# An FFT mixing layer and a GELU MLP on one core: batch 1's first stage packed closer, its filters reloaded around the read behind it, seven products in the last tile

## The chip, the cores and the metric

The kernel runs on one core of a Trainium2 chip. The metric is the device time of one execution in microseconds, the median of seven runs. Of the core's engines, PE multiplies matrices into PSUM, ACT (ScalarE) and DVE (VectorE) compute elementwise and move PSUM to SBUF, POOL (GpSimd) computes elementwise in SBUF and issues DMAs, and SP (SyncE) only issues DMAs and waits. Each engine runs its own instructions in the order in which the program wrote them; semaphores hold one until what it needs is there.

## What is computed

Two layers, one behind the other. The first mixes each of the 256 channels of eight sequences of 3008 positions with a filter in the frequency domain; the second is an MLP with an exact GELU on all 24064 positions.

```python
X = np.fft.rfft(x, axis=1)                 # x: 8 x 3008 x 256
Y = X * (filt_r + 1j * filt_i)[None]       # filters: 1505 x 256
y = np.fft.irfft(Y, n=3008, axis=1)
h = y.reshape(24064, 256) @ w_in           # 256 x 2048
g = 0.5 * h * (1.0 + erf(h / sqrt(2)))
out = g @ w_out                            # 2048 x 256
```

## The kernel before

**The Fourier layer.** 3008 is 47 x 64, so a sequence goes through four stages of small matrix products. Stage one (`s1`, four calls c = 0 to 3, "bursts", L380) multiplies x by a 47-point table, moves four PSUM banks into a tile `a` (three by DVE, one by ACT in batch 1) and writes it to DRAM with four DMAs of 96 KB (`R1`, L402; the profile shows `R<-a_sb`). `r1` (L404) reads it back transposed as `b`: c = 0 to 2 together, c = 3 later. Stage two (`s2`, twelve calls p = 0 to 11) multiplies by a twiddle table and by the filters `F` (L419, on DVE, for both filter parts; call p uses filter rows 2p and 2p+1): the products `p12`. Stage three (`s3`, `s3_out`) goes back to DRAM (`R2`, L445), `r2` reads `d` (L452), and stage four (`s4`, sixteen calls, table `T4a`) leaves y in SBUF, in a ring of two sequences. Batch 0 does the same in forms of its own (`c1` to `c4`, L470 to L556) with its filters in another order; so the filters are loaded and copied into the upper partitions (`dup_filters`, L115), saved to DRAM (`save_filters`, L97) and loaded again in the later batches' order (`load_filters_again`, L108: eight DMAs a call, on SP).

**The MLP.** The output is cut into 47 tiles of 512 positions, and a tile into 16 slots. In slot s of tile t PE does a sixteenth of the first matrix product (`mm1`, two matmuls of 512 columns, L575), which ACT turns into one of the 16 parts of `g` with GELU (L578), and a sixteenth of the second product of tile t - 1. For the first and the last tile that is `mm2` (L580): 64 matmuls of 256 columns a tile; the last tile's fourth part is done in two halves of 128 columns, so that little is left to store at the end. For all others it is `mm2_seven` (L647), which saves an eighth of the columns: the 2 x 2 blocks of g and w_out are combined so that seven products of 256 x 1024 x 128 do instead of eight, each of 16 matmuls of 128 columns, seven matmuls a slot. For that DVE makes sums of g: `sums_1` (four calls, L632), `sums_2` (two, L638, into a quarter of g itself) and `sums_3` (two, L645), in slots given in the last lines of the program; the third product (m = 2) uses what sums_2 wrote, the fourth and fifth use sums_1's and the seventh sums_3's. DVE adds the products in L675 to L685, and SP stores.

**What sets the order.** The order on every engine is written by hand. `put(slot, f, ...)` hangs work of the Fourier layer on slots, counted from the first slot of tile 0; a slot's `put` work comes ahead of its `mm2` and `mm1`. In slots 0 to 15 there is no second product yet, and a slot is two matmuls; from slot 16 on it is both. For batch 1 the numbers stand in one line:

```python
s1, n1, r1, s2, n2, group, r2, s4, n4 = 0, 4, 15, 22, 2.5, 12, 59, 67, 0.75   # L837
unit = lambda p: s2 + group * (p // 4) + int(n2 * (p % 4))                  # L840
```

Bursts are in slots s1 + n1 c, reads of b in slot r1, s2 call p in slot unit(p) (22, 24, 27, 29, 34, ...), s4 call u in slot s4 + int(n4 u). Other `put` work of the first tile: the factors of table 4 (three small matmuls and three evacuations by ACT, L354) in slot 7, `table_4_all` (L367: POOL builds T4a from them in 24 operations) in slot 11, the sums of w_out for the seven products (`weight_sums`, DVE, L612) and the second reload of filters (rows 8 to 23) in slot 17.

**Buffers.** `a` has 3, `b` 3, `p12` 6, `d` 3, `ost` (stores, and the accumulators of the seven products) 4. PSUM has eight banks: h (3: mm1, and one bank of a burst), o (2: second product), f (3: the rest of the Fourier stages).

## Time and profile before

| what | us |
|---|---|
| median of 7 runs | 752.85 (751.95 to 753.65) |
| the profiled execution | 752.35 |
| its span, first to last instruction | 750.6 |
| PE busy | 729.7 (97% of the span) |
| DVE busy | 585.8 (78%) |
| ACT busy | 545.4 (73%) |
| POOL busy | 100.9 (13%), nearly all before 72 us |
| slot 0 (first burst) on PE | 38.4 |
| slot 16 | 50.9 |
| slot 22 (first call of s2) | 59.6 |
| first matmul of the last tile's second product | 740.6 |
| last matmul | 747.6 |
| last store issued | 748.1 |

A group's line in the profile gives engine, line, operation, output tile, input tiles, shapes, and how many; behind it, in brackets, the idle time before it and what ended that. A line of the waits gives total, number of times and the longest. The granted clock of PE was full throughout.

### The profile page before, as it was taken

The numbers are of one execution on the slowest core, as the hardware profiler recorded it, in microseconds if no ns is written. First come the engines' busy times: TensorE is split into PE (matmuls) and PEld (weight loads), VectorE is DVE, ScalarE is ACT, GpSimd is POOL, SyncE is SP. The second block draws the span as 40 slices with busy tenths as digits, with TensorE's granted clock in tenths as the row PEclk, the third lists the DMA queues.
The fourth block names the chain that finished last, engine by engine and source line by source line (L and its number), as shares of the span: only waits on it lengthen the run. The fifth ranks groups of instructions, "written<-read, shape, count | busy, mean of one in ns | idle before, by whom it ended". The sixth has DMA issues, their size and how long they took to land.

```text
span 750.6 us, 20037 instructions
## 1 busy us (share of the span) xinstructions
PE 729.7 (97%) x8252; PEld 518.0 (69%) x8388; DVE 585.8 (78%) x1051; ACT 545.4 (73%) x963; POOL 100.9 (13%) x191
## 2 busy tenths in 40 slices
PE   8988999999999999999999999999999999999998
PEld 4835676766776667666677667666677766777776
DVE  8958978898787977789777997779967798666562
ACT  7875678767786677866777667876678767777773
POOL 7988000021001200012000120002100000000000
PEclk9999999999999999999999999999999999999999
DMA  9999563474445753547526456255562432501011
GB/s 151 232 206 249 144 141 93 116 167 105 113 103 146 143 131 78 143 137 136 123 83 172 107 112 166 57 152 120 121 147 72 135 106 73 127 29 58 30 57 57
DMA packets 91804, 90.71 MB, mean 121 GB/s; under 512 B 7744, under 2 KB 78528, under 8 KB 91456
## 3 DMA queue, kind: packets, MB, share of 16 engines
q1 hardware_dynamic: 83328, 73.43, 35.5%
q0 software_dynamic: 8384, 16.00, 14.4%
q8 instruction: 65, 1.06, 0.6%
q14 instruction: 27, 0.22, 0.1%
HBM read 57.15 MB, written 48.23 MB: 140 GB/s over the span
## 4 chain that ended last, share of the span: by engine, by line
PE 87%; DVE 5%; POOL 2%; issue 2%; DMA 2%; ACT 1%; SPq 0%; DVEq 0%; ACTq 0%; POOLq 0%
PE ps_o L662 37%; PE ps_h L575 36%; PE ps_s L461 3%; PE ps_s L433 3%; PE ps_s L416 3%; PE ps_s L392 2%; DVE p L419 2%; ACT g_sb L578 1%; PE ps_o L602 1%; DVE s_sb L632 1%; POOL t_sb L376 1%; DMA x_sb<-in_x_dram 1%; POOL T4a L378 1%; PE ps_c L523 1%; PE ps_c3t L538 1%
## 5 line engine op out<-in xcount | busy, mean ns | idle before, releaser
L578 ACT ACTIVATE g_sb<-ps_h 128x512 f16<-128x512 f32 x752 | 448.1, 598 | 184.4 <-PE ps_h L575 162.4
L575 PE MATMUL ps_h<-y_sb,w_in_sb 128*128 128x512 bf16 (+3 forms) x1468 | 417.9, 365 | 1.8 <-DVE a_sb L302 1.7
L662 PEld LDWEIGHTS <-g_sb 128*128 128x128 f16 x2880 | 190.1, 98 | 78.8 <-issue 15.6
L662 PEld LDWEIGHTS <-s_sb 128*128 128x128 f16 x2160 | 147.5, 98 | 51.3 <-issue 2.9
L575 PEld LDWEIGHTS <-w_in_sb 128*128 128x128 bf16 x1600 | 124.6, 98 | 8.5 <-issue 3.4
L662 PE MATMUL ps_o<-w_sums,s_sb 128*128 128x128 f16 x1440 | 124.5, 219 | 1.3
L662 PE MATMUL ps_o<-w_sums,g_sb 128*128 128x128 f16 x1440 | 124.7, 219 | 0.8
L662 PE MATMUL ps_o<-w_out_sb,g_sb 128*128 128x128 f16 x1440 | 118.4, 219 | 1.8
L632 DVE TENSOR_TENSOR s_sb<-g_sb 128x1024 f16<-128x1024 f16 x180 | 119.2, 685 | 0.0
L419 DVE TENSOR_TENSOR p<-ps_s,F 128x1024 bf16<-128x1024 f32 x84 | 102.4, 1220 | 17.8 <-PE ps_s L416 16.8
L123 POOL COPY gate<-p 1x1 bf16<-1x1 bf16 x40 | 19.1, 477 | 423.9 <-DVE p L419 423.9
L662 PE MATMUL ps_o<-w_out_sb,s_sb 128*128 128x128 f16 x720 | 62.2, 219 | 0.5
L638 DVE TENSOR_TENSOR g_sb<-s_sb,g_sb 128x1024 f16<-128x1024 f16 x90 | 61.7, 685 | 1.1
L645 DVE TENSOR_TENSOR s_sb<-g_sb 128x1024 f16<-128x1024 f16 x90 | 61.3, 681 | 0.0
L304 DVE TENSOR_SCALAR y_sb<-ps_s 128x376 bf16<-128x376 f32 x56 | 30.5, 545 | 28.7 <-PE ps_s L461 28.7
L302 DVE CAST a_sb<-ps_s 128x512 bf16<-128x512 f32 x60 | 38.5, 685 | 17.4 <-PE ps_s L392 13.9
L461 PEld LDWEIGHTS <-d_sb 96*128 96x128 bf16 x448 | 31.4, 98 | 26.8 <-DMA d_sb<-R 1.2
L680 DVE TENSOR_TENSOR t_sb<-t_sb,ps_o 128x256 f32<-128x256 f32 x45 | 18.7, 416 | 39.7 <-PE ps_o L662 39.7
L677 DVE TENSOR_TENSOR ost<-t_sb,ps_o 128x256 f32<-128x256 f32 x45 | 18.8, 418 | 31.3 <-PE ps_o L662 31.3
L461 PE MATMUL ps_s<-T4a,d_sb 96*128 96x94 bf16 x448 | 37.4, 206 | 2.2 <-DMA d_sb<-R 0.7
L685 DVE TENSOR_TENSOR ost<-t_sb,ps_o 128x256 f32<-128x256 f32 x90 | 33.5, 414 | 7.4 <-PE ps_o L662 7.4
L416 PE MATMUL ps_s<-b_sb,T2p 128*128 128x256 bf16 x168 | 32.1, 273 | 2.9 <-POOL T4a L378 1.9
(149 smaller groups left out, 514.0 us busy)
## 6 DMA issues: line engine op xcount, KB each, us to landing
out_dram<-ost SPq DMA_DIRECT2D x93, 256.0 KB, 2.8
x_sb<-in_x_dram POOLq DMA_DIRECT2D x64, 188.0 KB, 3.9
R<-a_sb SPq DMA_DIRECT2D x112, 96.0 KB, 2.2
b_sb<-R SPq DMA_DIRECT2D x28, 384.0 KB, 4.4
R<-v_sb SPq DMA_DIRECT2D x84, 128.0 KB, 2.4
d_sb<-R SPq DMA_DIRECT2D x56, 192.0 KB, 4.1
F<-Fd SPq DMA_DIRECT2D x8, 256.0 KB, 8.4
Fd<-F SPq DMA_DIRECT2D x8, 192.0 KB, 7.0
```

The costliest lines, as they stand in the source:

```text
L302: self.nc.vector.tensor_copy(out=out, in_=in_)
L304: self.nc.vector.tensor_scalar(out=out, in0=in_, scalar1=scale, scalar2=None, op0=ALU.mult)
L416: nc.tensor.matmul(ps[:, 256 * i:256 * i + 256], lhsT=self.T2p[:, k].rearrange("p a b c d -> p (a b c d)"), rhs=self.st[b, "b", k // 6][:, ...
L419: nc.vector.tensor_tensor(out=w, in0=ps.unsqueeze(1).to_broadcast([128, 2, 512]), in1=self.F[:, :, 2 * p:2 * p + 2, :].rearrange("p t a b ...
L461: nc.tensor.matmul(ps[:, 94 * i:94 * i + 94], lhsT=d[:, (grp % 2) * 4 + i, 128 * half:128 * half + 128], rhs=self.T4a[:, 4 * grp + i], sta ...
L575: nc.tensor.matmul(ps[:, o:o + n], lhsT=self.w_in_sb[:, dc, jc * 128:jc * 128 + 128], rhs=self.ring[:, dc, off:off + n], start=(dc == 0), ...
L578: nc.scalar.activation(out=self.st["g", t][:, jc, :], in_=ps, func=AF.Gelu)
L632: self.nc.vector.tensor_tensor(out=self.st["s", t][:, i:i + 2], in0=a, in1=b, op=ALU.subtract)
L638: self.nc.vector.tensor_tensor(out=a21[:, k], in0=self.st["s", t][:, k, 0], in1=a22[:, k], op=ALU.add)
L645: self.nc.vector.tensor_tensor(out=self.st["s4", t][:, k], in0=a12[:, k], in1=s2[:, k], op=ALU.subtract)
L662: nc.tensor.matmul(ps[:, (m + 1) % 2, sub, :], lhsT=a[:, i, 128 * sub:128 * sub + 128], rhs=b[:, i], start=i == 0, stop=i == 7)
L685: v(out=c(h, 1 - h), in0=tt, in1=p, op=ALU.add)
```

## The change

It has four parts.

1. Batch 1's bursts are hung on slots 0, 3, 6 and 9 instead of 0, 4, 8 and 12, and the read of b on slot 12 instead of 15. The last burst writes into two buffers of the product ring `p12` (two halves of 1024 elements) instead of a tile `a`. s4 starts in slot 68 instead of 67, with 0.68 instead of 0.75 slots a call, so that the last call stays in slot 78.
2. The first reload of filters (rows 0 to 7, eight DMAs of 128 KB, issued during batch 0) is split in two calls of four rows (eight DMAs of 64 KB each) in slots 11 and 13, one ahead of the read of b and one behind it. The factors of table 4 move from slot 7 to 12, table U and `table_4_all` from slot 11 to 13.
3. In batch 0 the copies of filter rows 4 to 23 (POOL) and the saves (SP) stand later in the program; rows 0 to 3 are copied by DVE alone (before: two by ACT, two by DVE), and the second half of the first evacuation of `c1t` goes to ACT.
4. The last tile uses the seven products as well. Its results are stored in pieces: a quarter after the third product, one after the fifth, and the sixth and seventh products in halves, each with a bank, an addition (`finish`) and a DMA of 64 KB of its own.

```diff
 def s1(self, b, c):
-        a = self.pa.tile([128, 2, 4, 256], BF16, tag="a", name="a_sb")
+        if b == 1 and c == 3:
+            a = [self.pp.tile([128, 2, 512], BF16, tag="p12", name="p12").rearrange("p i (j c) -> p (i j) c", j=2)
+                 for h in range(2)]
+        else:
+            a = self.pa.tile([128, 2, 4, 256], BF16, tag="a", name="a_sb")
+            a = [a[:, 0], a[:, 1]]
...
 def mm2(self, t, s):
-        last = t == self.B * self.S // TCH - 1
-        if last and tile_i == 3:
...
-        if last and s == 11:
-            self.store(t, 2, ps[:, 0, :], slice(0, 256))
-        elif s % 8 == 7:
+        if s % 8 == 7:
...
 def mm2_seven(self, t, s):
+        last = t == self.B * self.S // TCH - 1
         for n in range(7 * s, 7 * s + 7):
             m, sub, i = n // 16, n // 8 % 2, n % 8
-            if n % 16 == 0 and (m == 0 or m % 2 == 1):
-                self.st["o"] = self.bank("ps_o", "o").rearrange("p (m s o) -> p m s o", m=2, s=2)
+            if n % 16 == 0 and (m == 0 or m % 2 == 1) or last and m > 4 and i == 0:
+                self.st["o"] = self.bank("ps_o", "h" if n > 80 else "o").rearrange("p (m s o) -> p m s o", m=2, s=2)
...
-            if n % 16 != 15 or m % 2:
+            if last and m > 4 and i == 7:
+                self.finish(t, m, sub, ps)
+            if n % 16 != 15 or m % 2 or last and m > 4:
                 continue
...
             elif m == 2:
                 v(out=c(0, 0), in0=t1, in1=p0, op=ALU.add)
+                if last:
+                    self.store(t, 0)
                 v(out=t1, in0=t1, in1=p1, op=ALU.add)
             elif m == 4:
                 v(out=t3, in0=t1, in1=p0, op=ALU.subtract)
                 v(out=c(1, 1), in0=t3, in1=p1, op=ALU.add)
+                if last:
+                    self.store(t, 1)
                 v(out=t1, in0=t1, in1=p1, op=ALU.add)
...
+    def store(self, t, h):
+        r0, k = t * TCH + 256 * h, slice(128 * h, 128 * h + 128)
+        self.nc.sync.dma_start(out=self.out[r0:r0 + 256, k].rearrange("(s p) o -> p s o", p=128),
+                               in_=self.st["c"][h][:, :, k])
+
+    def finish(self, t, m, sub, ps):
+        h = 6 - m
+        c, tt = self.st["c"][h], self.st["t"][:, h]
+        k = slice(128 * (1 - h), 128 * (1 - h) + 128)
+        self.nc.vector.tensor_tensor(out=c[:, sub, k], in0=tt[:, sub], in1=ps[:, (m + 1) % 2, sub], op=ALU.add)
+        r0 = t * TCH + 256 * h + 128 * sub
+        self.nc.sync.dma_start(out=self.out[r0:r0 + 128, k], in_=c[:, sub, k])
...
     nc.gpsimd.memset(m.vt[:, :, 96, :], 0.0)
-    m.dup_filters(nc.gpsimd, 4, 20)
-    for k in (12, 0):
-        m.save_filters(k, 12)
...
     m.table_3(1)
-    m.dup_filters(nc.scalar, 0, 2)
+    m.dup_filters(nc.vector, 0, 4)
+    m.warm_up(1)
+    m.c1t(0, (False, act))
     m.table_3_copy(1, False)
-    m.dup_filters(nc.vector, 2, 2)
-    m.warm_up(1)
-    m.c1t(0, (False, False))
+    m.dup_filters(nc.gpsimd, 4, 20)
+    for k in (12, 0):
+        m.save_filters(k, 12)
...
-            if q == 2:
-                m.load_filters_again(0, 8)
...
-            s1, n1, r1, s2, n2, group, r2, s4, n4 = 0, 4, 15, 22, 2.5, 12, 59, 67, 0.75
+            s1, n1, r1, s2, n2, group, r2, s4, n4 = 0, 3, 12, 22, 2.5, 12, 59, 68, 0.68
...
-    put(7, m.table_4_factors, g)
-    put(11, m.table_u)
-    put(11, m.table_4_all, g)
+    put(12, m.table_4_factors, g)
+    put(13, m.table_u)
+    put(13, m.table_4_all, g)
+    put(11, m.load_filters_again, 0, 4)
+    put(13, m.load_filters_again, 4, 4)
     put(17, m.load_filters_again, 8, 16)
...
-    seven = range(1, NT - 1)
+    seven = range(1, NT)
```

## The prediction

> **What bounds the kernel now.** I read the page first: PE is busy for 97% of the span, and in the row of 40 slices only the first few are below 9. So I went to the waits of PE over the whole span; the stalls of batch 0's tables (below 21 us) apart, four are long enough to matter.
>
> ```profile
> PE ps_s L416 <- POOL T4a L378: 1.9, 1, 1.9
> PE ps_h L575 <- DVE a_sb L302: 1.7, 1, 1.7
> PE ps_o L602 <- DMA w_out_sb<-in_moe_w_out_dram: 1.2, 1, 1.2
> PE ps_s L461 <- DMA d_sb<-R: 0.7, 1, 0.7
> ```
>
> They add up to 5.5 us; from about 104 us on PE waits for nothing over 0.15 us. So the change can win only in the first 104 us and in the tail. The timeline of PE places the stalls: 1.69 before 50.06, 1.24 before 54.05, 1.92 before 59.60, 0.73 before 103.93. What lies behind them stands in the timelines of SP and DVE.
>
> ```profile
> 40.74 12.43 SPq L402 DMA_DIRECT2D R<-a_sb  x16
> 55.98 1.29 SPq L408 DMA_DIRECT2D b_sb<-R  x3
> 57.32 5.94 SPq L113 DMA_DIRECT2D F<-Fd  x8
> ```
>
> ```profile
> 49.32 1.89 DVE L302 CAST a_sb<-ps_s 128x512 bf16<-128x512 f32 x3 [3.40 <-DMA R<-a_sb]
> 54.10 0.69 DVE L618 TENSOR_TENSOR w_sums<-w_out_sb 128x1024 f16<-128x1024 f16 x1 [2.90 <-DMA w_out_sb<-in_moe_w_out_dram]
> 54.83 1.35 DVE L618 TENSOR_TENSOR w_sums<-w_out_sb,w_sums 128x1024 f16<-128x1024 f16 x1
> ...
> 64.80 1.23 DVE L419 TENSOR_TENSOR p<-ps_s,F 128x1024 bf16<-128x1024 f32 x1 [1.60 <-PE ps_s L416]
> 65.94 1.26 DVE L632 TENSOR_TENSOR s_sb<-g_sb 128x1024 f16<-128x1024 f16 x1
> 67.12 1.21 DVE L419 TENSOR_TENSOR p<-ps_s,F 128x1024 bf16<-128x1024 f32 x1
> 68.25 1.28 DVE L632 TENSOR_TENSOR s_sb<-g_sb 128x1024 f16<-128x1024 f16 x2
> ```
>
> The fourth burst's evacuation waits for a buffer until the first burst's writes have landed (49.2). The last write is issued at 52.9 and lands 3.0 later; only then, at 55.98, can the read of b be issued, which lands 3.5 later, at 59.5. That is the true end of the wait put down to T4a, which stage two does not read. The second half of w_out lands at 54.0 (34.3 and 19.7).
>
> **First stage: bursts every three slots, the last into product tiles.** ACT sets the pace of slots 0 to 15: its timeline is unbroken from 39.08 to 47.4, a GELU every 0.48 to 0.49 us. Its work is 16 x 0.485 + 4 evacuations x 0.50 + 0.52 (factors of table 4) + 0.15 (U) = 10.4, so without the buffer wait the last GELU starts at 39.08 + 10.4 - 0.5 = 49.0; it started at 51.22. Three slots of PE and a burst take 3 x 0.44 + 0.56 = 1.88, a burst's three casts on DVE 1.89: the denser bursts just fit. Gain **2.2** (1.7 if DVE falls behind). The tiles borrowed from the product ring cost nothing: their writes land some 20 us before products 4 and 5 want the buffers.
>
> **w_out.** Eight filter DMAs (1 MB), now issued at 30.3 to 33.6, land up to 45.1 among those of x, the last of which lands at 44.9. Taken out, x should be done near 39.5 (the first at 33.0, the other seven 0.93 apart, as batch 0's were) and w_out, at the 4.3 to 4.8 us a half that it took beside R's writes, near 48.6. Slot 18 wants it at 52.8 - 2.2 = 50.6: the whole **1.24** goes. With nothing gained in its landing, PE would wait 3.4 there.
>
> **The read of b.** Casts end at 38.83 + 4 x 1.89 = 46.4; four issues at 0.4 and a landing of 3.0, as the last one's, put the last write at 50.6. The eight small filter DMAs of slot 11 stand between on SP. SP's waits show later writes waiting for earlier ones (4.0 us, six times), which I read as eight in flight; so the eighth filter DMA follows the last write, and the read 0.4 to 1.2 behind it: issued near 51.6, landed at 55.1 to 55.5. PE arrives at 57.7 - 3.45 = 54.2 and waits about one microsecond. At slot 22 PE is **4.2** ahead (3.4 if the writes still land 0.9 apart, as beside w_out, 4.9 if the read is no hindrance).
>
> **What is late next: DVE.** From 64.80 (product 2) DVE works without a gap to the end of the second sums_2 of tile 1, at 73.59 + 0.67 = 74.26, and PE needs that at 74.86, the second matmul of the group at 74.80. That slack is 0.6 us. The trace shows what can break it: while POOL builds T4a (44.25 to 67.98), the subtractions and additions of two SBUF tiles on DVE take 1.26 to 1.35 in four of five cases, afterwards 0.67 or 0.68, one every 0.60. The change starts T4a later (its factors pass through ACT in slot 12, not 7): ACT gets to them at 39.08 + 12 x 0.485 + 4 x 0.50 = 46.9 and takes 0.52, so POOL starts near 47.5, 3.25 later, and is stretched in turn; it ends near 72 to 73, while DVE's work comes 4 us earlier. Five sums (two rows of the pair at 68.25, two L638, one L632) fall under POOL: 5 x 0.58 = 2.9. DVE starts product 2 at 60.8, ends sums_2 at 60.8 + 9.46 + 2.9 = 73.2, and PE resumes there at 73.2 instead of 74.8: of 4.2 there remain **1.6**. Bounds: 4.2 (no contention), 0.3 (also product 2 starting 1.3 late on its filters).
>
> [...]
>
> **Filters' return.** Products 2 and 3 need the second small reload, issued around the read; the third b lands about 3.4 behind the first, near 58.7, and at 250 GB/s (2 MB of the later reload from 62.9 to 71.4) 0.5 MB take 2.2: 60.8, just in time. The big reload follows, 8.4 more: 69.3 to 70. Product 4 wants it near 70.9 by the chain above (73.2 - 1.2 - 1.1). Cost 0, with a microsecond to spare.
>
> **Head.** POOL and SP keep the order of their own instructions, as nothing of theirs stands between the old and the new place of the filter copies and saves. DVE gains a copy of 0.42, ACT loses one of 1.04 and takes half of an evacuation; the first product waits for DVE's first half as before. 0, bounds -0.2 and +0.2.
>
> **Stage four a slot later.** Another slot of 0.82 covers the 0.73: **+0.65**, bounds 0 and 0.73.
>
> **Last tile.** PE: 48 x 0.109 + 32 x 0.056 = 7.0 becomes 112 x 0.056 = 6.2. But DVE has two sums_2 and a sums_1 behind 741.09, at 0.6 to 0.7 each, to 743.0, where PE wants the last at 740.58 + 36 x 0.056 = 742.6: 0.4 lost. The last product's additions queue behind three of 0.33 to 0.46, and SP has four issues of 0.33 to 0.35 in a row: the last leaves at about 748.1 to 748.2, before at 748.12, and lands 1.5 later. **+0.1**, bounds -0.3 and +0.7.
>
> Sum: 1.6 + 0 + 0.65 + 0.1 = 2.35. The profiled execution took 752.35 (span 750.6 and 1.75 around it); 750.0 in its terms. The median of the seven runs is 752.85, 0.5 above it, so I predict 750.5. About 0.2% (1.5 us) is what a measurement can tell from no change.
>
> **Rivals.**
> 1. The contention is small: POOL ends early or blocks few sums. Then 4.2 + 0.65 + 0.1 = 4.95 are won: 747.9. For it: the row at 54.10, 0.69 while POOL worked. Against: four others. Chance 0.22.
> 2. The gains of the first stage are used up at slot 37 (product 2 late on its filters and five sums slowed): 0.3 + 0.65 - 0.2, 752.1. For it: no slack in the DVE chain. Chance 0.22.
> 3. Slower: the filters decide. If small filter DMAs land 1.1 apart, as the eight between 35 and 45 did among x's, eight take 8.8 in place of 2.2, and the big reload lands at 58.7 + 8.8 + 8.4 = 75.9; product 4 (1.14) and sums_2 (0.67) behind it end at 77.8, where PE wanted 74.86: 2.9 lost, 0.75 won back: 755.0. It decides from 70.9 on, and the change loses from about 73.7 on. Against: nothing else moves data then. Chance 0.10.
>
> The forecast has 0.46 (its own range 749.3 to 751.4). Faster by over 0.2% are it, nearly whole, and the first rival: 0.66; within 0.2% the second and part of the third: 0.27; slower 0.07. The range takes in the first rival's time and most of the second's: 747.7 to 752.6.
>
> **What would show it.** No wait for a_sb before slot 13 and none for w_out at slot 18; the first b landing near 55; L632 and L638 at 1.2 to 1.3 up to 72 us, T4a ending there; a PE wait of 2 to 3 us at the second quarter of tile 1's third product (L662), near 71 to 73; no wait for d_sb. It is wrong if that wait is missing, if DVE waits for F before product 4, or if the read of b lands after 57.

## The result and the profile after

The change makes the kernel slightly slower. The median is 754.47 us over 24 runs (751.97 to 756.2); runs of the kernel before beside them have 753.23 (62 runs). The ratio is 1.0018, with a 95% interval of 1.0012 to 1.0024: 0.9 to 1.8 us lost where 2.35 were forecast as won. The profiled execution took 754.18, its span 752.4, so 1.85 of span more than before's. That is more than the medians differ by (1.24): before's profiled execution, 752.35, lies 0.9 below its median.

I begin, as before, with the waits of PE (total, times, longest):

```profile
PE ps_s L421 <- DMA b_sb<-R: 3.5, 1, 3.5
PE ps_warm L294 <- DVE turn_r L215: 1.4, 1, 1.4
PE ps_s L466 <- DMA d_sb<-R: 1.3, 2, 0.9
PE ps_o L653 <- DVE g_sb L628: 1.2, 2, 0.9
```

The waits for `a_sb` and `w_out` are gone, as they should be. But the wait for the read of b, 1.92 before, is now 3.46 long (the timeline's number). The table sets the start of a slot's GELU beside that of before; minus is ahead.

| slot, or place | after less before, us | what lies just ahead of it |
|---|---|---|
| 17 | -2.21 | denser bursts, no wait for `a_sb` |
| 21 | -3.60 | no wait for `w_out` |
| 22 | -1.84 | PE waits 3.46 for b (before 1.92) |
| 24 to 36 | -0.39 | two slots of 1.7 us in place of 0.87 to 1.08 |
| 37 | +0.68 | PE waits 0.89 for DVE (`sums_2`) |
| 67 | -0.63 | no wait for `d_sb` at 104 us |
| 74 to 440 | -0.28 | s4 ends in the same slot as before |
| 450 | +0.55 | PE waits 0.88 for `d_sb` at 463.7 |
| 550 to the last GELU | +0.88 | PE waits 0.47 for `d_sb` at 555 |
| end of the span | +1.85 | last GELU to end: 10.76, before 9.79 |

So upstream of slot 21 the change did what it was to do (0.23 of the 2.21 was there at slot 0 already), and nearly all of it is given back between slots 21 and 24. SP's timeline shows why b is late. A row gives start, length from the first issue to the end of the last, and the number of issues.

```profile
40.51 7.41 SPq L407 DMA_DIRECT2D R<-a_sb  x12
48.02 1.92 SPq L407 DMA_DIRECT2D R<-p  x4
49.99 3.71 SPq L113 DMA_DIRECT2D F<-Fd  x8
53.80 1.32 SPq L413 DMA_DIRECT2D b_sb<-R  x3
55.20 3.50 SPq L113 DMA_DIRECT2D F<-Fd  x7
```

The last write leaves at 49.49 and lands at 51.81. In between SP does not wait for it: SP issues the eight small filter DMAs of slot 11, one every 0.46 to 0.47 us, until 53.7. Only then comes the read, 2 us after the write that it needs has landed. It lands at 57.41. The timeline of PE shows the wait, and something else behind it:

```profile
53.49 0.59 PE L580 MATMUL ps_h<-y_sb,w_in_sb 128*128 128x512 bf16 x2
57.54 0.38 PE L421 MATMUL ps_s<-b_sb,T2p 128*128 128x256 bf16 x2 [3.46 <-DMA b_sb<-R]
57.76 0.60 PE L594 MATMUL ps_o<-w_out_sb,g_sb 128*128 128x256 f16 x4
58.19 0.82 PE L580 MATMUL ps_h<-y_sb,w_in_sb 128*128 128x512 bf16 x2
58.80 1.06 PE L594 MATMUL ps_o<-w_out_sb,g_sb 128*128 128x256 f16 x4
...
62.25 0.60 PE L594 MATMUL ps_o<-w_out_sb,g_sb 128*128 128x256 f16 x4
```

The same four matmuls take 0.60 at 57.76, 1.06 at 58.80 and 0.60 again at 62.25. The windows view names the cause in its third column from the right, the granted clock (behind the stretch stand busy time and count of PE, PEld, DVE, ACT, POOL; then clock, DMA share, GB/s):

```profile
56.00:57.00 1.00, 0.00 (x0) 0.00 (x0) 0.00 (x0) 0.00 (x0) 0.92 (x2) 1.00 1.00 384
58.00:59.00 1.00, 1.00 (x7) 0.54 (x5) 1.00 (x1) 0.00 (x0) 0.92 (x2) 0.71 1.05 377
59.00:60.00 1.00, 1.00 (x6) 0.61 (x4) 0.28 (x2) 0.60 (x1) 0.92 (x2) 0.50 1.01 228
61.00:62.00 1.00, 1.00 (x6) 0.68 (x5) 0.82 (x1) 0.35 (x1) 0.92 (x2) 0.58 0.87 209
62.00:63.00 1.00, 1.00 (x8) 0.68 (x7) 0.41 (x1) 0.55 (x1) 0.92 (x2) 1.00 0.98 279
```

PE ran at half clock from 58.43 to 61.84, 3.41 us, which cost 1.45 by the table. In the profile of before the clock was full throughout; but that is one execution, and not a usual one, as the section on the clock shows. On the page's row of 40 slices this can't be seen: each slice there is 19 us long.

DVE's timeline, behind product 2, shows the contention that was forecast:

```profile
65.55 1.17 DVE L622 TENSOR_TENSOR s_sb<-g_sb 128x1024 f16<-128x1024 f16 x1
...
67.77 2.47 DVE L622 TENSOR_TENSOR s_sb<-g_sb 128x1024 f16<-128x1024 f16 x2
...
71.36 1.17 DVE L628 TENSOR_TENSOR g_sb<-s_sb,g_sb 128x1024 f16<-128x1024 f16 x1
...
73.06 0.68 DVE L622 TENSOR_TENSOR s_sb<-g_sb 128x1024 f16<-128x1024 f16 x1
...
74.79 0.68 DVE L628 TENSOR_TENSOR g_sb<-s_sb,g_sb 128x1024 f16<-128x1024 f16 x1
```

Sums take 1.17 to 1.3 until POOL has built T4a, at 71.98, and 0.68 afterwards: four of them here, one in before's row of the same place. Last the tail, DVE's and SP's:

```profile
747.75 0.95 DVE L697 TENSOR_TENSOR ost<-t_sb,ps_o 128x128 f32<-128x128 f32 x4
```

```profile
748.06 1.85 SPq L699 DMA_DIRECT2D out_dram<-ost  x4
```

The last addition is done at 748.71, 0.26 earlier behind the last GELU than before's last copy. But the four stores leave SP 0.49 apart, the last one at 749.53, 0.8 after the addition that it stores. Behind the last GELU that is 7.87, before 7.34: 0.53 of the tail's 0.97. The rest stands behind the last issue; the run with two queues below shows where.

### The profile page after: what moved, and what is told of

It reads as the page before. It is cut to its first block, busy times and chain, and to the rows that moved or that the text cites. A ratio compares the mean times of both kernels' runs of the same rounds, so it can differ in the third digit from the quotient of the medians.

```text
span 752.4 us, 20124 instructions
## 1 busy us (share of the span) xinstructions
PE 730.1 (97%) x8284; PEld 519.1 (69%) x8420; DVE 593.2 (79%) x1065; ACT 544.7 (72%) x963; POOL 101.2 (13%) x191
## 3 DMA queue, kind: packets, MB, share of 16 engines
q8 instruction: 66, 1.08, 0.6%
## 4 chain that ended last, share of the span: by engine, by line
PE 85%; DVE 6%; DMA 4%; ACT 2%; issue 2%; SPq 1%; POOL 0%; DVEq 0%; POOLq 0%; ACTq 0%
PE ps_o L653 36%; PE ps_h L580 35%; PE ps_s L466 3%; PE ps_s L438 3%; PE ps_s L421 2%; PE ps_s L397 2%; DVE p L424 2%; ACT g_sb L583 1%; DVE s_sb L622 1%; DMA R<-v_sb 1%; DMA F<-Fd 1%; DMA d_sb<-R 1%; DMA x_sb<-in_x_dram 1%; PE ps_c L528 1%; DMA b_sb<-R 1%
## 5 line engine op out<-in xcount | busy, mean ns | idle before, releaser
L653 PEld LDWEIGHTS <-g_sb 128*128 128x128 f16 x2944 | 193.9, 98 | 80.7 <-issue 15.6
L653 PEld LDWEIGHTS <-s_sb 128*128 128x128 f16 x2208 | 150.2, 98 | 51.3 <-issue 2.9
L653 PE MATMUL ps_o<-w_sums,g_sb 128*128 128x128 f16 x1472 | 127.1, 219 | 2.0 <-DVE g_sb L628 1.2
L653 PE MATMUL ps_o<-w_sums,s_sb 128*128 128x128 f16 x1472 | 126.5, 219 | 1.3
L622 DVE TENSOR_TENSOR s_sb<-g_sb 128x1024 f16<-128x1024 f16 x184 | 122.9, 691 | 0.0
L653 PE MATMUL ps_o<-w_out_sb,g_sb 128*128 128x128 f16 x1472 | 120.3, 219 | 1.8
L628 DVE TENSOR_TENSOR g_sb<-s_sb,g_sb 128x1024 f16<-128x1024 f16 x92 | 63.5, 691 | 1.1
L635 DVE TENSOR_TENSOR s_sb<-g_sb 128x1024 f16<-128x1024 f16 x92 | 62.6, 681 | 0.0
L302 DVE CAST a_sb<-ps_s 128x512 bf16<-128x512 f32 x57 | 36.6, 685 | 13.0 <-PE ps_s L397 12.8
```

The lines of the kernel that those rows point to most:

```text
L302: self.nc.vector.tensor_copy(out=out, in_=in_)
L622: self.nc.vector.tensor_tensor(out=self.st["s", t][:, i:i + 2], in0=a, in1=b, op=ALU.subtract)
L628: self.nc.vector.tensor_tensor(out=a21[:, k], in0=self.st["s", t][:, k, 0], in1=a22[:, k], op=ALU.add)
L635: self.nc.vector.tensor_tensor(out=self.st["s4", t][:, k], in0=a12[:, k], in1=s2[:, k], op=ALU.subtract)
L653: nc.tensor.matmul(ps[:, (m + 1) % 2, sub, :], lhsT=a[:, i, 128 * sub:128 * sub + 128], rhs=b[:, i], start=i == 0, stop=i == 7)
```

## The experiments

Against each other stood two explanations. The first: the loss is made by the places that the trace shows, the late read with the half clock behind it, the sums under POOL, and the four issues of the tail; take one away and its time comes back. The rival: these places only pass time on; stage two can't run earlier, because the next thing (the later reload of the filters, buffers, the writes of stage three) is about as late, so that what one edit wins another wait takes. Times are medians, each beside runs of the kernel before on the same chip; a hundredth of a per cent is 0.075 us. "After" is the changed kernel. Apart from extra matmuls of ones in some of them, whose results nobody reads, all of them compute the same.

### Which part costs how much

**The tail alone, and all but the tail.** In one kernel the last tile is as before in the changed kernel; in the other, part 4 alone stands in the kernel before.

```diff
-    seven = range(1, NT)
+    seven = range(1, NT - 1)
...
```

> The changed kernel with the last tile as before (eight products, its last part in two halves, three stores). The trace of the changed kernel ends 110.7 us - 100 = 10.7 us after the last GELU's start, that of before 9.8: four stores of 64 KB are issued 0.49 apart on SP instead of 0.35 long with gaps. If that is the tail's whole story, this is 0.9 us faster than the changed kernel, 0.3 above the kernel before. Rival (as predicted): the tails are equal and the 0.9 belongs to something else; then nothing changes.

Measured: 1.0000 [0.9992, 1.0009], 753.79 beside 753.09; from the last GELU to the end 9.78, as before.

```diff
-    seven = range(1, NT - 1)
+    seven = range(1, NT)
...
```

> The kernel before with the seven products in the last tile alone. By the same reading 0.9 us slower than the kernel before (0.5 to 1.2); as predicted, 0.1 us faster (-0.3 to +0.7). The span behind the last GELU's start tells it: 10.7 or 9.8 us.

Measured: 1.0013 [1.0004, 1.0021], 754.63 beside 753.09; 10.98 from the last GELU to the end. Part 4 costs 1.0 us alone and 1.35 as the difference of the changed kernel's ratio and that without it (1.0018 less 1.0000): that is most of the loss, and what remains of the change wins nothing that can be told.

**The finishing stores on two queues.** If the row of issues on SP makes the tail long, half of them on ACT's queue should shorten it.

```diff
-        self.nc.sync.dma_start(out=self.out[r0:r0 + 128, k], in_=c[:, sub, k])
+        (self.nc.sync if sub else self.nc.scalar).dma_start(out=self.out[r0:r0 + 128, k], in_=c[:, sub, k])
```

> The kernel before with the seven products in the last tile, and of the four last stores the first half of each product issued from ACT's queue, the second from SP's. With all four on SP they left 0.49 apart and the last 0.8 after its addition was done; the end stood 10.7 to 11.0 behind the last GELU's start, with the old last tile 9.8. If SP's four issues in a row are the loss, two queues bring the end to 9.8 to 10.1: 0.6 to 0.9 faster than with all on SP, level with the kernel before within 0.3. If the loss is in the sums or the landing, it stays at 10.7.

Measured: 1.0003 [0.9994, 1.0013], 753.67 beside 752.81 (the base is the kernel with part 4 alone). The tail is 10.11 in place of 10.98. Two timelines, ACT's and SP's:

```profile
747.86 0.87 ACTq L694 DMA_DIRECT2D out_dram<-ost  x2
```

```profile
748.06 0.99 SPq L694 DMA_DIRECT2D out_dram<-ost  x2
```

With two issues on a queue the row is 1 us long, not 1.85 to 2.07. So most of the tail's loss, 0.87 of 1.19 in these profiles, is the row of issues (in the medians, 1.0003 against 1.0013, the gain is within noise). The remaining 0.3 lies behind the last landing. At the end SP waits for the landings of its DMAs on eight semaphores, one behind the other in a fixed order, 0.06 us apart, and the DMAs use these eight in turn. From the last store's landing on, in the kernel before and then in the changed one:

```profile
L906 SPq EVENT_SEMAPHORE  x1: 28/28/28, 749.7 to 749.7; - x1
```

```profile
L909 SPq EVENT_SEMAPHORE  x7: 27/28/28, 751.1 to 751.5; - x7
```

In the kernel before the last store happens to have the last semaphore of the row; with part 4 it has the second. From its landing to the end of the span it takes 0.91 or 0.92 in all thirteen profiles with the old last tile and 1.28 in all seven with part 4: 0.37 that has nothing to do with the arithmetic. A tail with another number of DMAs was not tried.

**Stage four a slot later, alone,** in the kernel before.

```diff
-            s1, n1, r1, s2, n2, group, r2, s4, n4 = 0, 4, 15, 22, 2.5, 12, 59, 67, 0.75
+            s1, n1, r1, s2, n2, group, r2, s4, n4 = 0, 4, 15, 22, 2.5, 12, 59, 68, 0.68
```

> The kernel before with stage four from slot 68 at 0.68 slots a call, alone. The wait for d of 0.73 at 103.9 goes: 0.65 us faster than the kernel before. In the changed kernel slot 67 won 1.24 against the kernel before and slots 68 to 74 gave 0.35 back, so 0.6 to 0.9. Rival: the wait only moves to a later read of d, and nothing changes.

Measured: 0.9994 [0.9986, 1.0003], 752.56 beside 752.80. In its profile slot 67 is 1.24 further ahead than slot 66; 0.18 of that is given back at slot 68 and 0.17 at 74, so 0.89 stands. The median shows half of it. This is the part that most likely wins, but its interval still takes in 1.

**The bursts without the moved reload.** The whole first reload goes back into batch 0; the last tile is as before.

```diff
+            if q == 2:
+                m.load_filters_again(0, 8)
...
-    put(11, m.load_filters_again, 0, 4)
-    put(13, m.load_filters_again, 4, 4)
```

> The changed kernel with the last tile as before and the small reload whole and early, as before (rows 0 to 7, eight DMAs among batch 0's products). The first reload then lands among x and w_out again: w_out's second half near 53 to 54, PE waits there 2 to 3 us; R's writes are done near 55 and b lands near 58.5. If the moved reload is what makes the bursts pay, this is 0.5 to 1.5 us slower than the same kernel with the moved reload, which was level with the kernel before; if the read of b comes at the same time with any order, it is equal to it or faster, since the wait is cut in two (w_out, then b) and the clock is kept.

Measured: 0.9993 [0.9985, 1.0001], 752.54 beside 753.33, the lowest ratio of all, and within noise that of stage four alone. The denser bursts, table 4's move and the head together come to nothing that can be told (each interval is 0.6 us either way): `w_out` lands late again (a wait of 0.70), the read of b is issued at 56.01, as before (55.98), and PE, which arrives earlier, waits for it:

```profile
PE ps_s L421 <- POOL T4a L378: 2.5, 1, 2.5
```

(The read lands at 59.23, PE goes on at 59.37; T4a is the same misattribution as in the profile before.) Behind it the clock is at half from 59.68 to 63.10.

**The moved reload without the bursts,** on top of stage four's slot.

```diff
-            if q == 2:
-                m.load_filters_again(0, 8)
...
+    put(14, m.load_filters_again, 0, 4)
+    put(16, m.load_filters_again, 4, 4)
     put(17, m.load_filters_again, 8, 16)
```

> The kernel before with stage four a slot later (0.24 faster by the median, 1.2 in its profile), and the small reload in slots 14 and 16 around the read of b in slot 15, bursts every four slots in the ring a. x and w_out land earlier (w_out near 47), so the first burst's writes do too, and the waits for a and for w_out shrink from 2.9 together to about 1; the read of b is held by eight issues, as in the changed kernel, and PE waits for it 3 us or more with the half clock behind. If the read's landing sets the front, the time stays level with the kernel before (-0.5 to +1); if the earlier x and w_out decide, 1 to 2 us faster.

Measured: 1.0020 [1.0010, 1.0030], 754.93 beside 753.33: 2.0 us worse than stage four alone (1.0020 less 0.9994). The waits for `a_sb` (0.75 is left) and `w_out` shrink or go, but eight issues again stand before the read:

```profile
51.79 3.70 SPq L113 DMA_DIRECT2D F<-Fd  x8
55.59 1.32 SPq L408 DMA_DIRECT2D b_sb<-R  x3
```

The read lands at 58.78, PE waits 3.90, and half clock follows from 58.78 to 62.19. Moving the reload frees the front and sends all that it frees into the same wait.

**The last burst in a tile `a`,** not in the product ring.

```diff
-        if b == 1 and c == 3:
+        if False:
```

> The changed kernel with the last burst in a tile of the ring a, as the others. Its casts then wait for the first burst's writes, which landed at 47.21 in the changed kernel while the casts began at 44.69: DVE and ACT stop for 2.5 us, PE for about 1.5 to 2 at slot 12, and the last writes leave near 50.5 instead of 49.5. If all lost time upstream is taken out of the wait for b, as the failure of the front suggests, the b wait shrinks by as much as the stall adds, the single wait over 3 us becomes two short ones and the half clock is gone: level with the changed kernel or up to 1.5 us faster. If the product tiles won what I predicted (1.7 to 2.2 to the end), it is that much slower than the changed kernel.

Measured: 1.0022 [1.0012, 1.0032], 754.46 beside 752.81; the changed kernel has 1.0018, so the borrowed tiles make no difference that can be seen. In its profile PE stalls 2.71 at 48.9 for `a_sb` (half clock from 47.79 to 54.62), and in exchange there is no wait of PE for b over 0.3 us: slot 22 stands at -0.19 of before. What is lost early is not lost again at the read. That fits both explanations; it says that the read is the place where all of the front's time is settled.

### Getting the read of b out earlier

**The first half of the small reload back among batch 0's products,** so that nothing stands between the writes and the read.

```diff
+            if q == 2:
+                m.load_filters_again(0, 4)
...
-    put(11, m.load_filters_again, 0, 4)
```

> The changed kernel with one edit: the first small reload of filters (rows 0 to 3, eight DMAs) goes back to where the reload stood before, among batch 0's products, so that nothing stands on SP between the last burst's writes and the read of b. If those eight issues hold the read (issued at 53.80 in the changed kernel, the last write having landed at 51.81), it is issued near 52.0 to 52.5 and lands near 55.5 to 56; PE waits 1.5 to 2 us at slot 22 instead of 3.46, and if the half clock from 58.43 to 61.84 comes of the length of that wait, it is gone too: about 3 us less up to slot 24, of which DVE's chain at slot 37 may take 1 to 2 back; 1 to 3 us faster than the changed kernel, 0 to -1.8 against the kernel before. Rival: the memory traffic decides and not the queue. Then the 0.5 MB put back ahead of x and w_out delay R's writes by about 2 us and the read lands at 57 as now; the time stays at that of the changed kernel, 1.2 us above the kernel before.

Measured: 1.0004 [0.9993, 1.0015], 753.62 beside 753.09, some 1 us better than after (1.0018) with the longer tail kept. But not by way of the read: the extra DMAs delay `w_out` (a wait of 0.66) and the writes, the last of which lands at 54.70 (51.81 in the changed kernel); the read leaves at 54.78, at once, and lands at 58.08. The changed kernel's landed at 57.41, but the two kernels that are the same as it up to slot 16, those with the old last tile (the later reload whole, and in two, below), have 59.57 and 58.06 in their profiles. So one profile tells this landing to no better than 2 us, and 58.08 is neither early nor late. PE waits 2.64, half clock follows. Taking the issues out of the way made the data late instead; why the median is better stays open.

**The same DMAs issued by ACT.**

```diff
-    put(11, m.load_filters_again, 0, 4)
+    put(11, m.load_filters_again, 0, 4, nc.scalar)
...
-                self.nc.sync.dma_start(out=self.F[o:o + 32, t, k0:k0 + k, :], in_=i)
+                (eng or self.nc.sync).dma_start(out=self.F[o:o + 32, t, k0:k0 + k, :], in_=i)
```

> The changed kernel with the last tile as before, and the first small reload (slot 11, eight DMAs) issued from ACT's queue instead of SP's; the same bytes at the same place of the program. In the changed kernel SP issued it from 49.99 to 53.28, one every 0.46, so the read of b went out at 53.80 although the last write had landed at 51.81. Theory 1, SP's issues ahead of the read hold it: the read goes out 0.2 to 0.4 after the last write's landing and lands about 1.6 earlier, near 55.8 to 56.8; PE waits 1.5 to 2.5 at slot 22 instead of 3.5 to 4.9 and the half clock behind it is gone in part of the executions. Against the same kernel with the reload on SP (level with the kernel before) up to 3 us by slot 24; what of it is left at the end depends on slot 37: 0 to 2 us faster. Theory 2, memory traffic sets the landing: the read lands at 57.4 to 58.7 as before, and the time stays level with the kernel before or grows by ACT's eight issues (0.4 each at most).

Measured: 1.0009 [1.0000, 1.0019], 753.76 beside 752.81; the base is the kernel with the old last tile. ACT's timeline:

```profile
46.53 4.70 ACTq L113 DMA_DIRECT2D F<-Fd  x8
51.28 0.60 ACT L583 ACTIVATE g_sb<-ps_h 128x512 f16<-128x512 f32 x1 [4.62 <-DMA F<-Fd]
```

ACT sits in its issues for 4.7 us, and no GELU runs. PE waits 4.23 for it at 51.93, with half clock from 50.77 to 57.6. The read now leaves at 53.63, just behind the last write's landing (53.48, 1.67 later than in the changed kernel), and lands at 56.77, earlier than in any other profile, though by 0.6 only, and there is no wait for it, because PE is late by then.

**The same with table 4 early and the later reload in two,** the second half in slot 31.

```diff
-    put(12, m.table_4_factors, g)
-    put(13, m.table_u)
-    put(13, m.table_4_all, g)
+    put(7, m.table_4_factors, g)
+    put(11, m.table_u)
+    put(11, m.table_4_all, g)
...
-    put(17, m.load_filters_again, 8, 16)
+    put(17, m.load_filters_again, 8, 8)
+    put(31, m.load_filters_again, 16, 8)
```

> The previous one with table 4 in its early slots, and the big reload cut in two, rows 8 to 15 in slot 17 and 16 to 23 in slot 31, behind the last read of b on SP, so that this read is not held by the second half (in the run where both halves stood in slot 17, PE waited 1.71 for stage two at 85.1). If slot 37 was held by the big reload and the sums under POOL, it now passes 1.5 to 3 us ahead of the kernel before, and with the stage-four slot 2 to 3.5 us are won in all. If the read of b alone sets the front, it is level with the previous one.

Measured: 1.0009 [1.0000, 1.0018], 753.68 beside 752.81. ACT holds PE for 5.40 at 53.65. The later half of the aim is met, the first half of the big reload is there at 67.0 and no wait is left at slot 37, but that doesn't pay for the front.

### The clock

**Matmuls of ones in the wait for b** (slot 22; 1.9 us of them).

```diff
+    put(22, keep_warm, 8)
```

> The changed kernel with eight matmuls of ones (512 columns, into a free bank, their result is not used) in slot 22 ahead of the first call of s2; they take about 1.7 us of the 3.46 us in which PE waits for b. If PE's clock is halved because it idled for 3.46 us, the granted clock stays at 1.00 throughout, slots 22 to 24 take 0.87 to 1.08 us each instead of 1.7, and 1.5 us are won by slot 24; DVE's chain (sums under POOL) takes up to 1.0 of it back at slot 37, as the PE wait there grows. So 0.5 to 1.5 us faster than the changed kernel. Rival: the half clock is something else that falls there by chance; then it still shows near 58 to 62, and the time stays or grows.

Measured: 1.0016 [1.0005, 1.0027], 754.66 beside 753.09: no better than after. In the profile (the slowest of the eleven executions, 757.17) the edit works where it stands. b lands later than in the changed kernel's profile (58.70), PE's wait is 1.84, the clock stays full, and 0.86 is kept from slot 24 to 36. Then PE needs `sums_2` at slot 37, and DVE stands at product 4, whose filters land at 74.83 (71.91 in the changed kernel). DVE's timeline and PE's:

```profile
75.11 1.23 DVE L424 TENSOR_TENSOR p<-ps_s,F 128x1024 bf16<-128x1024 f32 x1 [2.31 <-PE ps_h L580]
76.25 0.68 DVE L628 TENSOR_TENSOR g_sb<-s_sb,g_sb 128x1024 f16<-128x1024 f16 x1
```

```profile
76.99 0.82 PE L653 MATMUL ps_o<-w_sums,g_sb 128*128 128x128 f16 x6 [2.83 <-DVE g_sb L628]
```

(The wait of 2.31 is put down to a matmul that was long done; the filter's landing at 74.83 is what came last.) The wait of 2.83 brings half clock here instead, 6.83 us of it from 76.20, and slot 40 is 5.06 behind before. One execution, and the worst, but it shows the rival at work.

**The same in the kernel with the bursts alone.**

```diff
+    put(22, keep_warm, 8)
```

> The changed kernel without the moved reload and with the last tile as before (0.5 us faster than the kernel before, interval -1.1 to +0.1), and eight matmuls of ones in slot 22 ahead of stage two. In its profile PE waited 2.55 for b and had the half clock for 3.41 us. With 1.7 of the wait filled the clock stays full and PE is 1.5 us further at slot 24. If nothing else is late, 1 to 1.5 us faster than without; if DVE's chain and the big reload (landed at 71.2) set slot 37, the wait comes back there and it is 0 to 0.5 faster, or slower, as in the other two pairs.

Measured: 1.0010 [1.0001, 1.0019], 754.01 beside 753.33; without the matmuls of ones 0.9993. In this profile `w_out` came late (54.92; 53.14 without the matmuls of ones), and the front waited 2.89 for it at 54.96, with half clock from 55.11, before the matmuls of ones were reached.

**Matmuls of ones ahead of the wait for `a_sb`,** in the kernel before with stage four's slot.

```diff
+    put(14, keep_warm, 7)
```

> The kernel before with stage four a slot later (0.4 us faster, interval -1.1 to +0.2), and seven matmuls of ones (1.5 us, into a free bank) in slot 14, where PE waits for the first burst's writes: 1.69 us in one profile of that stage, 3.0 in three others, two of which had the half clock for 3.41 us behind it. With the wait filled the clock is kept in all executions: 0 to 1.7 us less in half of them, 0.3 to 0.8 in the median, so 0.6 to 1.2 faster than the kernel before. If a later wait takes it, no change from 0.4.

Measured: 0.9997 [0.9988, 1.0006], 752.55 beside 753.33. The profile has full clock and a span of 749.3, as has the same kernel without them. Nothing that can be told from none.

**The clock of every execution.** The mean granted clock of each execution is on record, not of the profiled ones alone. In the profiles 0.997 or 0.998 goes with one half window among the matmuls, 0.995 with two, 1.000 with none (0.999, which no profile has, is too much for one). With the matmuls of ones in slot 14 nine of eleven executions had 1.000; without them (stage four's slot alone) two of eleven. So they did keep the clock, and the time did not follow: 0.9997 and 0.9994. Of the 160 executions of the kernel before that ran beside these kernels, only 34 had 0.999 or 1.000, and their mean time is 752.93; that of the others is 753.18, 0.25 more, with an interval of 0.0 to 0.5. So the half clock is usual in the kernel before as well, and of the 1.45 us that it took in front in the profile after little reaches the end. That is the rival again.

**Two profiles of one front.** The kernel with part 4 alone and the one with stage four alone have the same front, that of before. In both PE waits 3.0 us for `a_sb` near 51 us. The first had half clock behind it, the second not. Windows of the first, then of the second:

```profile
51.00:52.00 1.00, 0.69 (x3) 0.34 (x3) 1.00 (x3) 1.00 (x4) 0.92 (x2) 0.86 1.26 232
52.00:53.00 1.00, 1.00 (x4) 0.46 (x3) 0.45 (x1) 0.77 (x3) 0.92 (x2) 0.50 1.11 273
```

```profile
51.00:52.00 1.00, 0.79 (x4) 0.38 (x4) 1.00 (x3) 1.00 (x4) 0.92 (x2) 1.00 1.17 280
52.00:53.00 1.00, 1.00 (x9) 0.65 (x7) 0.35 (x1) 1.00 (x3) 0.92 (x2) 1.00 0.81 204
```

The changes of the clock lie on a grid of 3.413 us in every profile that has them (58.43, 61.84 and, 202 windows on, 751.33 in the profile after), with another phase in each execution. Where the wait lay nearly within one window of the grid (PE busy 0.12 of it) the clock went to half for the next, where it was cut by a border (0.42 busy) it did not. The profile of before has 1.69 in this place, and three others of this front have 3.0.

### DVE, POOL and the later reload

**Table 4 early again** in the changed kernel (slots 7 and 11).

```diff
-    put(12, m.table_4_factors, g)
-    put(13, m.table_u)
-    put(13, m.table_4_all, g)
+    put(7, m.table_4_factors, g)
+    put(11, m.table_u)
+    put(11, m.table_4_all, g)
```

> The changed kernel with the factors of table 4 back in slot 7 and table U and the building of T4a in slot 11, as before. POOL is then done near 68.5 instead of 71.9, and of the five sums that ran beside it in the changed kernel's DVE chain (1.1 to 1.2 us apart instead of 0.60) two or three are free. Theory 1, the shared work of DVE and POOL sets slot 37: the PE wait of 0.89 there goes, 0.9 us faster than the changed kernel (0.3 above the kernel before). Theory 2, the big reload of filters sets it: it landed at 71.9 in the changed kernel, at 71.4 in the kernel before and at 72.1 and 74.8 in the two runs with other orders, whatever came ahead of it; product 4 then starts near 72.0 and PE gains at most 0.9 and typically nothing, since product 4 is not before 72.

Measured: 1.0009 [0.9999, 1.0019], 753.99 beside 752.80. The wait at slot 37 is gone, and the sums behind 69 us take 0.68: so it was POOL that made them slow. But product 4 now waits 0.47 for its filters, which land at 73.23, and the loads of the next x, which POOL issues when T4a is done, start earlier and meet stage three's writes: DVE then waits 1.68 for those writes at 83.98, and PE 0.86 at 89.5.

**The later reload in two,** with the old last tile.

```diff
-    put(17, m.load_filters_again, 8, 16)
+    put(17, m.load_filters_again, 8, 8)
+    put(17, m.load_filters_again, 16, 8)
```

> The changed kernel with the last tile as before, and the big reload cut in two (rows 8 to 15, then 16 to 23, eight DMAs of 128 KB each): products 4 to 7 need the first half alone, and it lands about 4 us earlier, near 67.5 to 68. Theory 2 (the filters set slot 37) expects the chain to be free of them, a shorter wait where the reload came late, and 0.5 to 1 us less than with the uncut reload, which is level with the kernel before: -0.5 to -1 against it. Theory 1 (DVE beside POOL sets it) expects no change from that: level with the kernel before.

Measured: 1.0008 [1.0000, 1.0017], 753.52 beside 752.80, within noise of the same kernel unsplit (1.0000 [0.9992, 1.0009]). A wait of 0.96 at slot 37 remains, with sums of 1.17 to 1.25 under POOL ahead of it, so filters were not what it waited for.

**That with table 4 early and matmuls of ones in slot 22.**

```diff
-    put(12, m.table_4_factors, g)
+    put(7, m.table_4_factors, g)
...
+    put(22, keep_warm, 8)
```

> The previous one, with table 4 back in its early slots and the eight matmuls of ones in slot 22. If the clock, the filters and the contention each hold a share, and one hides the next, only all three together show it: no half clock in slots 22 to 24 (1.5), no wait for F at product 4, few slowed sums: PE passes slot 37 two to three us ahead of the kernel before, with the stage-four slot another 0.3 to 0.6: -2 to -3.5 us against the kernel before. If the read of b alone sets the front (landing near 57.4 to 58.7), less: -1 to -2.

Measured: 1.0027 [1.0015, 1.0040], 754.62 beside 752.80. The profile keeps full clock all through, is 1.06 ahead at slot 36 and 0.53 at 37, and then meets waits of 1.71 at 85.1 (stage three's casts), 0.31 and 0.71: at slot 79 it is 1.95 behind.

**The same with the second half of the reload in slot 31, with and without the matmuls of ones.**

```diff
-    put(17, m.load_filters_again, 16, 8)
+    put(31, m.load_filters_again, 16, 8)
```

> The changed kernel with the last tile as before, table 4 in its early slots, the big reload cut in two with its second half in slot 31 behind the last read of b, and the eight matmuls of ones in slot 22. In the run with both halves in slot 17 PE passed slot 36 1.06 us ahead of the kernel before and lost it to a wait of 1.71 at 85.1, for stage two behind the last read of b. Without that wait: 1 us ahead at slot 36, 1.5 ahead with the stage-four slot; 1 to 2 us faster than the kernel before. If DVE has no room for it (its sums at 88 to 90 came late too in two runs), level with it.

```diff
-    put(22, keep_warm, 8)
```

> The previous one without the matmuls of ones. PE waits 3.4 to 4.3 us for b in one piece, its clock is granted at half for 3.41 us in most executions and 1.7 us are lost: 1 to 1.7 us slower than the previous one. If the clock only takes what a later wait would take anyhow, the two are equal.

Measured: 1.0026 [1.0014, 1.0038] with them (754.65 beside 753.33), 1.0017 [1.0006, 1.0029] without (754.77). The first is the clearest case for the rival: full clock in front, 1.27 ahead at slot 36, 0.88 at 37, and then, on DVE, SP and POOL:

```profile
84.90 0.69 DVE L302 CAST v_sb<-ps_s 128x512 bf16<-128x512 f32 x1 [4.03 <-DMA R<-v_sb]
```

```profile
72.72 15.31 SPq L450 DMA_DIRECT2D R<-v_sb  x8
```

```profile
69.97 4.17 POOL L86 DMA_DIRECT2D x_sb<-in_x_dram  x8
```

The writes of stage three, issued from 72.7 on, land at 84.6 to 85.4. x of the next batch (eight loads of 188 KB, issued from 69.97 on) was issued ahead of them, which I take for the reason. PE waits 2.52, has half clock from 85.27 to 88.68, and is 3.31 behind at slot 48. In the second the waits are 2.77 for b, 0.52 at slot 37 and 1.90 at 86.

## Why the prediction was wrong

By its own steps, with what each measured in the profile after:

| step | predicted | measured |
|---|---|---|
| first stage | 2.2 won by slot 17 | 2.21, of which 0.23 at slot 0 |
| `w_out` | 1.24 won | 1.39 (slot 17 to 21) |
| read of b | lands 55.1 to 55.5, PE waits about 1, 4.2 ahead at slot 22 | lands 57.41, waits 3.46, 1.84 ahead (in two more profiles of this front 58.06 and 59.57, waits 3.86 and 4.88) |
| (not in the sum) half clock | 0 | 1.45 lost at that place |
| sums under POOL | 2.6 of the lead lost at slot 37 | 1.07 lost, of a smaller lead |
| filters | 0; big reload lands 69.3 to 70 | lands 71.91, no wait of its own |
| head | 0 | slot 0 at -0.23; not told from x's landing |
| stage four | 0.65 won | 0.89 in the profile of it alone, 0.45 in the medians |
| last tile | 0.1 won | 0.97 lost in the profile; 1.0 to 1.35 in the medians |

**The step that failed is "The read of b", and in it the time at which the last write leaves SP.** The step lets the last burst's four writes go right behind their casts, 0.4 apart: the casts end at 46.4, the last write leaves at 47.6. The casts ended at 46.58, as reckoned, but the last write left at 49.49, 1.9 late. SP was still busy with the third burst's writes. The first write of all, issued at 40.51, had landed only at 45.60, while `w_out` was loading, and SP's ninth write was held until then (45.66), the tenth until the second had landed (46.56; 46.63). SP's waits from 38 to 50 us have it:

```profile
SPq L407 <- DMA R<-a_sb: 1.5, 2, 0.9
```

The step names these waits itself ("which I read as eight in flight", 4.0 us in six waits before) and in its main line charges nothing for them (0.8 in a bound). From the last write's issue to the read's it reckoned 4.0 (47.6 to 51.6) and 4.3 was measured, but for another reason: not the last write's landing (51.81) held the read, but the eight filter issues on SP, 0.46 apart. So the read left at 53.80, 2.2 late; its flight of 3.6 was as reckoned. The text's own mark, "It is wrong [...] if the read of b lands after 57", was met, in all three profiles of this front. Whatever stood where in the other kernels, the read landed between 56.8 and 60.1, before at 59.5. Of the 3.6 us won in front of it, only what the read comes earlier, 59.47 to 57.41, could be kept.

**The second part of that failure was no term at all.** In before's profile three stalls of 1.69, 1.24 and 1.92 cost their length. In the profile after, one stall of 3.46 cost 1.45 more at its place, because PE's clock fell: to half for 3.41 us, behind a window of 3.413 us (55.01 to 58.43) in which PE was busy for 0.26 of it. With part 4 alone a window with 0.12 had the same behind it, and waits of 2.5 to 2.9 halved the clock in some profiles (2.55 for b in the bursts without the moved reload) and left it in others (2.77 for b with the second half of the reload in slot 31 and no matmuls of ones). As a reason for the slower medians the half clock weighs little: most executions of the kernel before have it too, and end only 0.25 later than those without.

**The last tile was mis-sized:** 0.1 won, bounds -0.3 and +0.7, against 0.97 lost in the profile. The PE and DVE work was right: PE waits 0.33 for the last sums (0.4 reckoned), and the last addition is 0.26 earlier. The issues were taken at 0.33 to 0.35 apiece, the length of single ones; in a row of four they leave 0.49 apart, and the last leaves 0.53 later. Another 0.37 stands behind the landing, in SP's row of semaphores, for which the step has no term. With two queues the first of the two is gone.

**Right for the reasons given** were the first stage, `w_out`, the contention of DVE's sums with POOL (1.17 to 1.3 until 71.98, T4a's forecast end was 72 to 73), which the run with table 4 early bears out, and the sign of stage four. The contention's size was not right: from product 2 to the end of the second sums_2 DVE took 11.06, before 9.46, so 1.6 and not 2.9. Product 2 started at 64.41 where 60.8 was forecast, and so three sums more than before fell under POOL, not five; the PE wait at slot 37 was 0.89, not 2 to 3. A slowed sum took 0.5 to 0.6 longer (1.17 to 1.3 in place of 0.68), not a whole POOL step of 0.98. Whether a sum waits for the rest of a step or the two share, the rows don't tell.

**Luck.** The third rival's 755.0 lies near the measured 754.47, but not for its reason: it has the big reload land at 75.9 and DVE wait for it, and it landed at 71.91, with no wait. (Its 1.1 us between the landings of eight filter loads is 1.44 in the rows of before, 35.01 to 45.09.)

**The sum, in medians.** Stage four -0.45, the rest of the front without the moved reload 0 (0.9993 against 0.9994), the moved reload +0.5 (1.0000 against 0.9993), the last tile +1.35: +1.4, the 0.18% that was measured. It closes by construction, as each term is the difference of two of these ratios, and is no test. The ratios' intervals are 0.5 to 0.7 us either way, so a term below 1 us is not shown, only the tail's is; the moved reload costs 2.0 where it stands without the bursts. Of the two explanations each has its share. The tail is the first's: taken away, its time comes back. The front fits the rival: of the edits that took away the issues before the read, the half clock or the sums' contention, none brought the time below before's by more than the interval; the read, the big reload (71 to 75), and the writes of stage three behind x's loads take over from each other.

**Open.** The head (part 3) was not run alone. Nor was a kernel tried in which the writes of the last burst leave SP earlier, which is where the failed step was off. PE's waits for `d_sb` at 464 and 555 us, 1.35 together in the profile after, stand in most of the profiles with half clock before 63 us and not in those with full clock throughout; why a shift of the program should bring them was not tried. What counts as busy for the clock is not settled either: with the last burst in a tile `a`, a window with PE busy for 0.54, partly in the small matmuls of a burst, had half clock behind it, and so had one of 0.56 in batch 0's small matmuls (9.39 to 12.81, second half of the reload in slot 31, no matmuls of ones), where windows of 0.42 to 0.64 elsewhere had not; and one of 0.40 in that same profile, with the wait of 2.77, had not, where another of 0.40 had.

No version here beats the kernel before by more than its interval; the bursts without the moved reload (0.9993) and stage four alone (0.9994) come nearest.

## What to carry to other kernels

Before adding up what is won in front of a chain of DMAs, follow that chain (what the queue still has to issue and to wait for when the data are ready, last write, landing, every issue ahead of the read at the pace of a row of issues, 0.46 us apart here, read, landing) to its end: here PE arrived earlier and only waited longer there, 3.46 in place of 1.92. Don't gather small stalls of PE into one without a look at the granted clock behind it: one of 3.46 cost 1.45 more at its place here, though little of that reached the end. At the end of a program count the issues on the last queue and what stands behind the last landing, not only the arithmetic, and try the issues on two queues (0.87 off the tail of a profile here, within noise in the medians). And look at the granted clock of all executions before taking a profile for the usual one.

## What the runs showed of the hardware

- The granted clock changed on a grid of 3.413 us in these profiles: in the one after it was full for 51.2 us (15 windows) up to 58.43, half for 3.413 and full for 689.5 (202 windows); half stretches in the others were 3.41 (59.68 to 63.10 in the bursts without the moved reload) or 6.83 long (47.79 to 54.62 with the last burst in a tile `a`). Its phase differed from one execution to the next, and the same wait of 3.0 us did (part 4 alone) and did not (stage four alone) halve the clock. Windows at full clock with PE busy for 0.00 (the moved reload without the bursts) to 0.33 had half clock behind them, all of them; of two at 0.40 one had; from 0.42 up (0.42, 0.49 and 0.64 in the profile of before) all but two, 0.54 and 0.56, had not. (Windows already at half clock stayed there at 0.66, 0.67 and 0.77.) From these counts I estimate that a wait needs about 2 us in one window (0.58 of it) to halve the clock.
- In a row, filter loads left SP 0.46 us apart and stores of 64 KB 0.49 (both in the profile after); filter loads with a pause before them took 0.30 (at 58.40 and 60.04 there), such stores 0.33 to 0.35 (in before's tail). ACT, given eight filter loads to issue, did nothing else for 4.7 us (46.53 to 51.23).
- In the profile after, while two loads of `w_out` were under way, a write of 96 KB took 5.1 us to land (40.51 to 45.60); the last of the same row, 2.3 (49.49 to 51.81).
- SP's waits at the end of the program stood 0.06 us apart, one for each of the eight semaphores that its DMAs used in turn: 0.37 us more where the last store had the second of the eight (1.28 from landing to end, seven profiles) than where it had the last (0.91 or 0.92, thirteen profiles).
